# Rearranging the operands of a fused attention, MoE and soft-MoE kernel for 38 prefetch slots

## The chip, the cores and the metric

One core of a Trainium2 chip runs the whole program. The metric is the device time of one execution in microseconds. Its engines are TensorE (PE; its weight loads stand apart as PEld), VectorE (DVE), ScalarE (ACT), GpSimd (POOL) and SyncE (SP), which here issues every transfer. Sixteen DMA engines move the data.

## The reference

Attention over queries pooled in pairs, a two-layer network with ELU on its result, and a soft mixture of eight experts on that (shapes: 4 batches, 8 heads, 1152 positions of 64; 512 model columns; w_in 512 x 2048; phi 512 x 32; w1 8 x 512 x 1024; w2 8 x 1024 x 512):

```python
q_pool = q.reshape(B, H, S // 2, 2, D).mean(axis=3)
attn = softmax(q_pool @ k.T / sqrt(D)) @ v          # to x: 2304 tokens x 512
h = x @ w_in
x = where(h > 0, h, exp(minimum(h, 0)) - 1) @ w_out
logits = x @ phi                                    # 2304 x 32
d = softmax(logits, axis=0)
slot_input = (d.T @ x).reshape(8, 4, 512)           # 4 slots for each expert
for e in range(8):
    slot_out[e] = maximum(slot_input[e] @ w1[e], 0) @ w2[e]
out = softmax(logits, axis=1) @ slot_out.reshape(32, 512)
```

## The kernel before

The kernel does not issue its work directly. Every step is given to a planner (`Plan.add`) with a due time, the engines that may do it, an estimated duration and the buffers it reads and writes. `Plan.run` then deals all steps out: at each turn it takes, of the steps that could start earliest on an engine, the one with the lowest rank (due time plus an offset from `PRI` for its class). What comes out is one fixed program order for each engine; on the chip every engine follows its order and waits on semaphores. A step's class name is phase, buffer name and engine: `1AtaPE` are the token transposes of the last batch (L1038), `1BlgPE` the logits of the last batch (L909).

The work has three phases. *Attention* (phase 0) runs over 16 pairs of heads, until about 427 us. *The two-layer network* (phase 1) consists of 32 products n, each a weight group w with a batch b: n = 0 to 23 run over groups 0 to 7 with batches 0, 1, 2 each, n = 24 to 31 over groups w = 8 to 15 (the same weights again) with batch 3. A product has two halves: `h_mm` (L851, w_in, four blocks of 12 matmuls on psA), then ELU on ACT and DVE, then `o_mm` (L890, w_out, eight groups of 6 matmuls, whose sums DVE adds to X at L901). All groups of a product sum on psC; of the last product (n = 31) four of the eight sum on psA. Each operand is split into a high and a low part. The w_in parts of even w lie in wi, of odd w in wj; the w_out parts of even w in wo, of odd w in wp. H and L are rings of five buffers for the parts of ELU's result; xh and xl the parts of X.

After batch 3 come its logits (L909), column maximum and exponentials, token transposes (L1038, copied into XN tiles by ACT and DVE), the product with the tokens (L1042), and the slot inputs (L1322). `combine` makes, batch by batch, the row softmax (DN), its split C3 (L1084 to L1086) and 20 transposes into C3T (L1105).

*The experts* (phase 2): the weights are 64 blocks of 512 KB, called units: 32 of w1 (rows of 4 KB), then w2, whole for the first experts (rows of 2 KB) and by column halves for the last `NLAST` = 2 (rows of 1 KB; first all of column half m = 0, then m = 1). `load_e` issues a unit on SP (L1215). `stage1` multiplies four w1 units at a time (L1230), `stage2` the w2 units (L1266). `finish(m)` makes column half m of the output: L1279, then nine pairs of token tiles (L1297), scaled into OSB by DVE (L1304) or ACT (L1302), and output transfers (L515) of six tiles each.

The on-chip memory is cut by hand: memr, memf, memv stay, and memy and memz are given up at a swap and taken again as memyq and memzq, once all their earlier users are done. A *slot* is a place of 512 KB for a unit; `spare` declares slots in space that has become free, each with a due time. The first units take the slots in the order of due times; later units (reloads) take them again in turn. Before, there are 29 slots: 4 in memyq, 4 in RAW, 2 each in X0, X1, and X2 (X2 once only), 4 in WR, and 11 in memzq. memy holds x parts of batch 0 alone in phase 1 and is swapped at product 22; memz holds wo, wj, wp, the low part of wi and the parts of batches 1 and 3, and is swapped behind the last L890.

Of the kernel before, what the change touches and what calls it, by code (L numbers as in the profile page):

```python
# [50 lines left out]
class Plan:  # L51
# [66 lines left out]
    def run(self):  # L118
# [54 lines left out]
        for _ in range(n):  # L173
# [41 lines left out]
            if e == "SP":  # L215
                bus = max(st + d + 1.6, bus) + ops[i][7] / 260e3
                end[i] = bus + 0.6
# [34 lines left out]
PRI = {'1AtaPE': -5.3608, '1LTDVE': -0.4594, '1RTDVE': -7.6429, '2SO*': -0.4526, '1MSACT': -0.9307, '1DN*': 8.8491, '2DNACT': 0.2194, '1wph*': -4.7823, '2BePE': -2.9011, '2erSP': -2.9653, '1EmACT': 4.7478, '1wih*': -3.2155, '1SIDVE': -16.5066, '2yqSP': 2.4557, '1Llg*': -8.1331, '2GPool': 3.2101, '2GDVE': -7.1, '2CDVE': 4.4865, '1PH*': 6.0485, '1xn*': -2.6051, '2SELDVE': 3.5395, '2MDVE': -0.6846, '1xl*': 0.61, '1scroSP': 1.1261, '1DRDVE': -0.4279, '2SOP*': -4.7028, '1xnDVE': 0.4531, '2SIZDVE': 6.7579, '1PHDVE': -0.095, '1Lm*': 5.0157, '2zqSP': -4.2858, '2BsitPE': -5.2295, '1BlgPE': 2.9402, '1X*': -1.2546, '2BsoPE': -9.6495, '1BtaPE': 4.0529, '1MSDVE': -5.9118, '2SODVE': 2.4582, '1wil*': -1.2109, '2AePE': -1.6771, '2SIZPool': -1.8218, '2CPE': 0.3788, 'PMXDVE': 5.8326, '0zSP': 5.8562, '0phiSP': 2.4789, '0UA*': -0.3377, 'PnmACT': 7.2492, '0ONERPool': 2.0662, '0qhACT': 0.8522, '0TMPDVE': -0.5015, 'PKRSP': 2.8555, '0QRSP': 2.4444, 'PMZDVE': 0.1661, '0khACT': 3.538, '0RAWACT': -0.5107, '0ACC*': 1.3624, 'PNQDVE': -2.7745, '0SMSP': 1.1984, '0rscrSP': -1.2373, '0scriSP': -4.5893, '0RBSP': 3.284, 'PqhACT': -3.9283, '0NQ*': 0.8442, '0qlDVE': -4.8402, '0KRSP': -0.8079, '0EAACT': 1.6723, 'PkhACT': 4.0482, '0nmACT': 1.1685, '1AhPE': -5.4283, '1wjh*': -0.2497, '1xh*': -9.449, '1woh*': -13.1407, '1wjl*': 1.9459, '1Hlg*': 1.9084, '1Hm*': -1.551, '1XN*': 1.3572, '1scriSP': -0.3405, '1SI*': 5.0824, '1AoPE': -3.7062, '1LT*': -1.0977}  # L252
# [17 lines left out]
OGRP = 6  # L270
# [12 lines left out]
NLAST = 2  # L283
# [3 lines left out]
def attention_moe_softmoe(  # L287
# [65 lines left out]

    def bank(tok):
        return psB[plan.phys[("B",) + tok]]
# [5 lines left out]
    SIZE = {"r": 15232 - 2 * KD * NQ, "f": 24456, "v": ND, "y": KD * NQ * 2, "z": 7 * ND + 2 * KD * NQ}  # L361
# [30 lines left out]
    Hr = [v3(x, 2) for x in carve("r", "H#", 5, NQ)]  # L392
    Lr = [v3(x, 2) for x in carve("r", "L#", 5, NQ)]
# [32 lines left out]
    BW = {("i", 0, x): carve("vz"[x == "l"], "wi" + x, 1, ND, late=True)[0] for x in "hl"}  # L426
    BW.update({("o", 0, x): carve("z", "wo" + x, 1, ND, late=True)[0] for x in "hl"})
# [10 lines left out]
    C3 = carve("r", "C3", 1, len(NT5) * 3 * NS)[0]  # L438
    XN = [v3(x, 2) for x in carve("r", "XN", 1, 2 * DM)]
# [416 lines left out]
    def elu(n, f, t):  # L856
        A, uk, ek, hk, lk = (("A", "h", n, f), ("E", "m", n, f), ("U", "m", n, f), ("H", "m", n, f), ("L", "m", n, f))

        def ph():
# [7 lines left out]
        add(t + 2, ("ACT", "DVE"), (act(NQ), dve2(NQ)), lambda e: copy_(got(Hr, hk), got(Ef, uk))(e), r=[uk], w=[hk])  # L867
        add(t + 2.6, ("DVE", "Pool"), (dve(NQ), pool(NQ)),
            lambda e: sub_(got(Lr, lk), got(Ef, uk), r32(got(Hr, hk)))(e), r=[uk, hk], w=[lk] + ([("elu", f)] if n == NSLOT - 1 else []))

    def o_mm(n, c, t, t0):
# [46 lines left out]
    def logits_split(b, t0):  # L918
        A = ("A", "lg", b)
        for c in range(KD):  # L920
# [4 lines left out]
            def mm(c=c, hk=hk, lk=lk):  # L925
                for x in (got(Hr, hk), got(Lr, lk)):
                    for t in range(2):
                        nc.tensor.matmul(got(psA, A)[: 2 * NS, t, :NH], lhsT=PH[:, c], rhs=x[:, t],
                                         start=(c == 0 and x is got(Hr, hk)), stop=(c == KD - 1 and x is got(Lr, lk)))

            add(t0 + c, ("ACT", "DVE"), (act(NQ), dve2(NQ)), lambda e, src=src, hk=hk: copy_(got(Hr, hk), src)(e), r=xr, w=[hk])
            add(t0 + c + 0.7, ("DVE", "Pool"), (dve(NQ), pool(NQ)),
                lambda e, src=src, hk=hk, lk=lk: sub_(got(Lr, lk), src, r32(got(Hr, hk)))(e), r=xr + [hk], w=[lk])
# [52 lines left out]
    def tok_all(b, t, dt):  # L986
# [38 lines left out]
        add(tq + 1.3, ("ACT", "DVE"), (0.26, 0.24), lambda e: copy_(dn(), pb()[:, :, NS:])(e), r=[tb], w=DK)  # L1025
# [134 lines left out]
    SIZ = over("f", "SIZ", 1, KD * NE * MQ, "LT")[0]  # L1160
    HS = over("f", "HS", 2, HF, "LT", 0, KD * NE * MQ)
    G = over("f", "G", 1, NE * 8 * MQ, "E#")[0]
    SOP = over("f", "SOP", 2, HM, "E#", 0, NE * 8 * MQ)
    SEL = over("f", "SEL", 1, 3 * NS, "E#", 0, NE * 8 * MQ + 2 * HM)[0]
    SO3 = over("r", "SO3", 2, HM, "H#", 0, 4 * ND)
    OSB = v3(over("f", "OSB", 1, NT * HM, "X", 2)[0], NT)
# [5 lines left out]
    def spare(kind, lo, avail, count=1, one=False):  # L1172
        for i in range(count):
            key = (f"er{len(slots_e)}", 0)
            off = lo + i * ND
            plan.region(key, BASE[kind] + off, BASE[kind] + off + ND)
            if one:
                once.add(len(slots_e))
# [11 lines left out]
    spare("z", 0, ts(32.55), 11)  # L1190
# [5 lines left out]
    onek = {f"er{x}" for x in once}  # L1196
# [6 lines left out]
    def load_e(u):  # L1203
# [11 lines left out]
        add(tm + 0.01 * u, "SP", 0.45, lambda: nc.sync.dma_start(v3(t(), a), src), w=[key] + ([("loads", 0)] if u == len(units) - 1 else []), size=524e3)  # L1215
# [4 lines left out]
    def stage1(u, t):  # L1220
# [3 lines left out]
        for i in range(2):  # L1224
# [46 lines left out]
    def finish(m, t):  # L1271
        so, sop = SO3[m], SOP[m]
# [102 lines left out]
```

## Time and profile before

| | us |
|---|---|
| median of 3 runs (lowest, highest) | 997.66 (996.82, 1002.28) |
| the profiled execution | 997.68 |
| its span, first to last instruction | 995.6 |
| PE busy in it | 958.6 |
| DVE busy | 760.4 |
| ACT busy | 496.9 |
| POOL busy | 396.3 |
| read from memory, written | 100.27 MB, 13.18 MB |

Shares of busy time are averages over stages with different limits, so the tail is read by stage. Rows of the timeline give a start, a duration (from the first to the last of a merged run of equal instructions), engine, line, what is written and read, the shape, the count, and in brackets the idle time before it and what ended that. Ends of pipelined matmuls are modelled, so starts are the firmer numbers. Rows of busy time by stage give the stretch, its length, the busy time and instruction count of PE, PEld, DVE, ACT and POOL in it, the clock granted to TensorE (as a share), the mean busy share of the DMA engines, and the GB/s that they moved. Rows of the chain and of the waits say so where they stand.

### The profile page before, as it was taken

What the parts mean: (1) busy time and instruction counts of PE and PEld (TensorE: products, weight loads), DVE (VectorE), ACT (ScalarE), POOL (GpSimd) and SP (SyncE); (2) the same over time, 40 slices, a digit from 0 to 9 for tenths busy, and PEclk for the clock granted to TensorE, in tenths of its full rate; (3) what the DMA queues carried; (4) which work ended last, traced back from release to release, by engine and by line L of the source; (5) the groups of instructions that cost most, each with busy time, mean ns of one, the idle gap of its engine ahead of it and who ended that gap; (6) DMA issues with size and microseconds to landing.
All of it is one profiled execution on the core that took longest, in us unless ns stands there. A gap on an engine that the chain in (4) does not pass through costs nothing.

```text
span 995.6 us, 20896 instructions
## 1 busy us (share of the span) xinstructions
PE 958.6 (96%) x8474; PEld 783.5 (79%) x8474; DVE 760.4 (76%) x1281; ACT 496.9 (50%) x887; POOL 396.3 (40%) x278
## 2 busy tenths in 40 slices
PE   7999999999999999999999999999999999998965
PEld 5777767766777777766899999999999999996423
DVE  6677798888888787899998989989758887765103
ACT  2555566555666566566664444443434475442102
POOL 2878888798888888897200000000000000000000
PEclk7999999999999999999999999999999999998996
DMA  7133424223334342202362332334330132315797
GB/s 175 45 86 85 106 73 122 72 78 113 85 85 116 85 105 61 88 16 67 105 201 89 104 121 95 107 99 162 139 116 28 43 127 86 123 47 230 288 377 267
DMA packets 101583, 114.86 MB, mean 115 GB/s; under 512 B 43632, under 2 KB 70768, under 8 KB 101488
## 3 DMA queue, kind: packets, MB, share of 16 engines
q1 hardware_dynamic: 101488, 113.55, 37.3%
q8 instruction: 66, 1.08, 0.4%
q14 instruction: 29, 0.24, 0.1%
HBM read 100.27 MB, written 13.18 MB: 114 GB/s over the span
## 4 chain that ended last, share of the span: by engine, by line
PE 85%; DVE 8%; DMA 4%; ACT 1%; SPq 1%; issue 1%; DVEq 0%; ACTq 0%
PE psC L890 20%; PE psA L851 20%; PE psC L690 14%; PE psA L683 10%; PE psS L683 5%; PE psA L614 3%; PE psS L614 3%; DVE memf L623 2%; DMA memf<-in_moe_w_dram 2%; PE psC L714 1%; PE psA L598 1%; PE psA L1230 1%; DMA memzq<-in_moe_w_dram 1%; PE psA L575 1%; DVE memf L557 1%; PE psC L659 1%
## 5 line engine op out<-in xcount | busy, mean ns | idle before, releaser
L704 POOL TENSOR_TENSOR memf<-memf 128x576 f32<-128x576 f32 x241 | 360.1, 1496 | 61.4 <-ACT memf L695 35.2
L890 PE MATMUL psC<-memr,memz 128*128 128x288 f32 x1512 | 224.7, 297 | 1.2 <-DVE memf L901 0.7
L890 PEld LDWEIGHTS psC<-memr,memz 128*128 128x128 f32 x1512 | 208.1, 188 | 4.4 <-ACT memf L509 1.6
L690 PE MATMUL psC<-memf 128*64 128x288 f32 x1152 | 174.2, 419 | 0.0
L695 ACT ACTIVATE memf<-psA 128x576 f32<-128x576 f32 x206 | 132.8, 651 | 63.0 <-PE psA L614 54.8
L623 DVE TENSOR_REDUCE memf<-psA 128x2 f32<-128x384 f32 (+3 forms) x235 | 142.5, 618 | 27.6 <-PE psA L614 14.1
L1335 POOL MEMSET memf<- 128x2048 f32 x1 | 1.8, 1809 | 388.4 <-DVE memr L512 388.4
L901 DVE TENSOR_TENSOR memf<-psC,memf 128x288 f32<-128x288 f32 x220 | 100.3, 463 | 47.6 <-PE psC L890 46.0
L623 DVE TENSOR_REDUCE memf<-psS 128x4 f32<-128x768 f32 (+1 forms) x140 | 103.5, 740 | 38.3 <-PE psS L614 20.5
L690 PEld LDWEIGHTS psC<-memf 128*64 128x64 f32 x1152 | 69.8, 136 | 48.6 <-issue 9.3
L851 PE MATMUL psA<-memz 128*128 128x288 f32 x512 | 93.8, 295 | 0.0
L862 ACT ACTIVATE memf<-psA 128x576 f32<-128x576 f32 x64 | 41.8, 652 | 102.8 <-PE psA L851 102.8
L509 ACT CAST memr<-memf 128x576 fp32r<-128x576 f32 x72 | 48.2, 674 | 74.4 <-PE psC L890 35.9
L851 PEld LDWEIGHTS psA<-memz 128*128 128x128 f32 x512 | 76.6, 188 | 0.0
L683 PE MATMUL psA<-memr 64*128 64x288 f32 x816 | 72.1, 299 | 1.8 <-DVE memf L623 1.8
L695 ACT ACTIVATE memf<-psS 128x576 f32<-128x576 f32 x82 | 53.4, 651 | 40.9 <-PE psS L614 35.4
L512 DVE TENSOR_TENSOR memr<-memf,memr 128x576 fp32r<-128x576 f32 x80 | 62.8, 791 | 6.4 <-ACT memr L509 5.9
L683 PEld LDWEIGHTS psA<-memr 64*128 64x128 f32 x816 | 59.1, 185 | 8.6 <-issue 3.9
L683 PE MATMUL psA<-memy 64*128 64x288 f32 x624 | 61.5, 302 | 0.0
L851 PE MATMUL psA<-memz,memv 128*128 128x288 f32 x256 | 52.0, 296 | 0.0
L683 PEld LDWEIGHTS psA<-memy 64*128 64x128 f32 x624 | 47.7, 188 | 4.1 <-issue 3.5
L509 ACT COPY memf<-psC 128x288 f32<-128x288 f32 (+1 forms) x66 | 26.2, 397 | 49.3 <-PE psC L1266 26.7
(209 smaller groups left out, 1602.5 us busy)
## 6 DMA issues: line engine op xcount, KB each, us to landing
memf<-wscr SPq DMA_DIRECT2D x32, 512.0 KB
memf<-in_moe_w_dram SPq DMA_DIRECT2D x30, 512.0 KB
memzq<-in_moe_w_dram SPq DMA_DIRECT2D x22, 512.0 KB
memz<-in_q_dram SPq DMA_DIRECT2D x32, 288.0 KB
memz<-in_k_dram SPq DMA_DIRECT2D x32, 288.0 KB
memf<-in_v_dram SPq DMA_DIRECT2D x16, 576.0 KB
memf<-in_moe_w_in_dram SPq DMA_DIRECT2D x32, 256.0 KB
wscr<-memf SPq DMA_DIRECT2D x32, 256.0 KB
```

The lines of the kernel that those rows point to most:

```text
L509: return lambda e: nc.scalar.copy(out_, in_) if e == "ACT" else nc.vector.tensor_copy(out_, in_)
L512: return lambda e: ENG[e].tensor_tensor(out_, a, b, ALU.subtract)
L614: nc.tensor.matmul(tile_[:m, j, lo : lo + n * MW], lhsT=qkb["qh", i][js, o : o + m], rhs=qkb["kh", i][js, g * MW : (g + n) * MW], start=Tr ...
L623: add(t, "DVE", dve(2 * n * MW), lambda: nc.vector.reduce_max(MX[i][:m, a, :, g : g + n], v4(got(psS, tok)[:m, :, lo : lo + n * MW], n), a ...
L683: nc.tensor.matmul(sp[:, j, :NH], lhsT=qkb[w, i][js, cs] if w else ONER[js], rhs=qkb[m, i][js, hs], start=(x == 0), stop=(x == 3))
L690: nc.tensor.matmul(psC[h][j * D : (j + 1) * D, :NH], lhsT=VR[i][:, j, c], rhs=e[:, j], start=(c == 0), stop=(c == NC - 1))
L695: add(t + 0.01, "ACT", act(NQ, True), lambda: nc.scalar.activation(got(EAf, E_), got(psS, S_)[:, :, :NH], AF.Exp, scale=1.0 / 16.0), r=[S_ ...
L704: ENG[e].tensor_tensor(ac, a, got(EAf, E_), ALU.add)
L851: nc.tensor.matmul(ph[:, t, :NH], lhsT=a, rhs=x, start=(i == 0), stop=(i == 3 * KD - 1))
L862: add(t, "ACT", act(NQ, True), lambda: nc.scalar.activation(got(Ef, uk), ph(), AF.Relu, scale=-1.0), r=[A], w=[uk])
L890: nc.tensor.matmul(po_(), lhsT=a, rhs=x, start=(i == 0), stop=(i == 3 * GF - 1))
L901: add(t0 + 0.8, "DVE", dve(NH), lambda: nc.vector.tensor_tensor(d, po_(), d, ALU.add), r=[ck], w=XK)
```

## The change

- The memory is cut anew. memy grows to 14 slots and holds, in phase 1, the parts of batches 0, 1 and 3 and wi's low part, wo and wj; memz shrinks and holds wp and the rings H and L. memyq is swapped with a due time behind the last w_in product (`YSW` = 31.2) and gives 14 slots, memzq 7. One more slot lies beside G in the E buffers, two (once only) in X3: 38 in all.
- DN of batches 0 to 2 moves into LT, C3T's space is shared with the last batch's XN tiles, HS and SOP move.
- The output gets a buffer for each column half (OS0 over X2 and X3, OS1 in memzq) and other transfer sizes: up to tiles 2, 6, 12, 18 for m = 0, and 6, 12, 16, 18 for m = 1.
- `NLAST` = 4: four experts by column halves, 16 half units instead of 8.
- `PRI` puts the last batch's logits ahead of its token transposes. In the planner, loads of phase 2 count 0.67 of their size instead of 0.75, and steps on SP without bytes no longer take up the bus.

```diff
-PRI = {'1AtaPE': -5.3608, ... '1BlgPE': 2.9402, ...
+PRI = {'1AtaPE': 4.0, ... '1BlgPE': -4.0, ...
-OGRP = 6
+OGRP = [[2, 6, 12, 18], [6, 12, 16, 18]]
-NLAST = 2
+NLAST = 4
+YSW = 31.2
...
-    SIZE = {"r": 15232 - 2 * KD * NQ, "f": 24456, "v": ND, "y": KD * NQ * 2, "z": 7 * ND + 2 * KD * NQ}
+    SIZE = {"r": 15232 - 2 * KD * NQ - 10 * NQ, "f": 24456, "v": ND, "y": KD * NQ * 4 + 5 * ND, "z": 2 * ND + 10 * NQ}
...
-    Hr = [v3(x, 2) for x in carve("r", "H#", 5, NQ)]
-    Lr = [v3(x, 2) for x in carve("r", "L#", 5, NQ)]
+    zo = 2 * ND
+    Hr = carve("z", "H#", 5, NQ, off=zo, late=True)
+    Lr = carve("z", "L#", 5, NQ, off=zo + 5 * NQ, late=True)
...
-    BW = {("i", 0, x): carve("vz"[x == "l"], "wi" + x, 1, ND, late=True)[0] for x in "hl"}
-    BW.update({("o", 0, x): carve("z", "wo" + x, 1, ND, late=True)[0] for x in "hl"})
...
-    BW.update({("i", 1, x): carve("z", "wj" + x, 1, ND, late=True)[0] for x in "hl"})
+    BW = {("i", 0, x): carve("vy"[x == "l"], "wi" + x, 1, ND, late=True)[0] for x in "hl"}
+    BW.update({("o", 0, x): carve("y", "wo" + x, 1, ND, late=True)[0] for x in "hl"})
+    BW.update({("i", 1, x): carve("y", "wj" + x, 1, ND, late=True)[0] for x in "hl"})
     BW.update({("o", 1, x): carve("z", "wp" + x, 1, ND, late=True)[0] for x in "hl"})
-    XH[1], XL[1] = (carve("z", f"x{x}1", 1, KD * NQ, late=True)[0] for x in "hl")
+    XH[1], XL[1] = (carve("y", f"x{x}1", 1, KD * NQ, late=True)[0] for x in "hl")
...
-        kind, off = ("v", 0) if i == 0 else ("r", plan.base[("H#", 0)][0] - BASE["r"] + (i - 1) * 2 * DM)
+        kind, off = ("v", 0) if i == 0 else ("r", plan.base[("C3T", 0)][0] - BASE["r"] + (i - 1) * 2 * DM)
...
-    OSB = v3(over("f", "OSB", 1, NT * HM, "X", 2)[0], NT)
+    OS0 = v3(over("f", "OS0", 1, NT * HM, "X", 2)[0], NT)
+    plan.region(("OS1", 0), BASE["z"] + oz, BASE["z"] + oz + NT * HM)
...
-    swap("y", y_es, "yq", ts(22.2))
-    spare("y", 0, ts(22.3), 4)
+    swap("y", y_es, "yq", ts(YSW))
+    spare("y", 0, ts(YSW + 0.05), 14)
...
     swap("z", z_es, "zq", ts(32.5))
-    spare("z", 0, ts(32.55), 11)
+    spare("z", 0, ts(32.55), 7)
+    spare("f", pos("E#") + NE * 8 * MQ, ts(32.5), r=[("elu", 0), ("elu", 1)])
+    spare("f", pos("X", 3), tm2 + 9, 2, True)
```

## Rows read from the trace of the kernel before

**Rows 1.** The page: DMA share (tenths) and GB/s of 40 slices.
```profile
DMA  7133424223334342202362332334330132315797
GB/s 175 45 86 85 106 73 122 72 78 113 85 85 116 85 105 61 88 16 67 105 201 89 104 121 95 107 99 162 139 116 28 43 127 86 123 47 230 288 377 267
```

**Rows 2.** Busy time by stage, columns as told under the table above.
```profile
440.00:480.00 40.00, 37.85 (x352) 28.38 (x349) 37.35 (x36) 26.25 (x46) 31.46 (x19) 1.00 0.12 41
...
920.21:925.83 5.62, 4.91 (x36) 2.41 (x38) 2.11 (x8) 1.59 (x7) 0.00 (x0) 0.90 0.14 56
...
938.00:978.00 40.00, 29.73 (x286) 13.53 (x287) 3.25 (x21) 3.45 (x11) 0.00 (x0) 0.89 1.01 358
978.00:995.60 17.60, 7.88 (x51) 5.41 (x49) 7.64 (x13) 6.13 (x15) 0.00 (x0) 0.69 0.79 268
```

**Rows 3.** The chain that ended last, from 923 on: start us, us, what.
```profile
936.16 10.76 DMA memf<-in_moe_w_dram
...
964.08 9.55 DMA memf<-in_moe_w_dram
```

**Rows 4.** Timeline of SP from 735 on.
```profile
905.21 7.39 SPq L1215 DMA_DIRECT2D memzq<-in_moe_w_dram  x11
925.83 1.75 SPq L1215 DMA_DIRECT2D memyq<-in_moe_w_dram  x4
...
979.24 10.42 SPq L515 DMA_DIRECT2D out_dram<-memf  x6
```

**Rows 5.** Busy time by stage again, for its last columns, DMA share and GB/s.
```profile
915.21:920.21 5.00, 4.49 (x11) 2.10 (x11) 1.16 (x5) 2.56 (x12) 0.00 (x0) 0.50 1.03 414
...
980.00:985.00 5.00, 3.53 (x25) 2.60 (x21) 3.55 (x7) 2.44 (x7) 0.00 (x0) 1.00 0.94 315
...
990.00:994.40 4.40, 0.00 (x0) 0.00 (x0) 0.00 (x0) 0.00 (x0) 0.00 (x0) 0.50 0.96 329
```

**Rows 6.** Timeline of PE from 955 on: expert products and what they waited for.
```profile
963.45 1.06 PE L1266 MATMUL psC<-memzq,memf 128*32 128x256 f32 x12 [0.73 <-DMA memzq<-in_moe_w_dram]
...
966.17 1.06 PE L1266 MATMUL psC<-memzq,memf 128*32 128x256 f32 x12 [0.74 <-DMA memzq<-in_moe_w_dram]
967.68 0.64 PE L1266 MATMUL psC<-memyq,memf 128*32 128x256 f32 x8 [0.45 <-DMA memyq<-in_moe_w_dram]
...
973.67 1.08 PE L1266 MATMUL psC<-memf 128*32 128x256 f32 x8 [0.71 <-DMA memf<-in_moe_w_dram]
```

**Rows 7.** Timeline of PE from 885 on: the last products of the network.
```profile
889.26 1.76 PE L851 MATMUL psA<-memz 128*128 128x288 f32 x12
890.86 1.75 PE L890 MATMUL psC<-memr,memz 128*128 128x288 f32 x12
...
896.08 0.97 PE L890 MATMUL psA<-memr,memz 128*128 128x288 f32 x6
...
898.55 1.06 PE L890 MATMUL psC<-memr,memz 128*128 128x288 f32 x6 [0.70 <-DVE memf L901]
899.45 0.97 PE L890 MATMUL psA<-memr,memz 128*128 128x288 f32 x6
```

**Rows 8.** Timeline from 905 to 947: tokens, slots and C3 on PE and DVE.
```profile
905.01 1.03 PE L1038 MATMUL psA<-ident,memf 128*64 128x128 f32 x8
...
920.36 1.29 PE L1105 MATMUL psB<-ident,memr 128*96 128x128 f32 x4
...
923.89 1.92 PE L1230 MATMUL psA<-memyq,memf 128*32 128x512 f32 x16
...
942.10 0.32 DVE L1084 CAST memr<-memf 128x160 fp32r<-128x160 f32 x1 [1.71 <-PE psB L1105]
...
945.07 1.36 PE L1105 MATMUL psB<-ident,memr 128*96 128x128 f32 x4
```

**Rows 9.** Waits of SP (us in all, times, longest); a DVE row.
```profile
SPq L515 <- DVE memf L1304: 15.7, 6, 8.2
...
985.68 1.29 DVE L1304 TENSOR_TENSOR memf<-psA,memf 128x512 f32<-128x512 f32 x2 [0.18 <-DMA out_dram<-memf]
```

More of the change, by code (lines that the diff above doesn't have):

```diff
@@ L214, in run @@
                 port = st + d
-            if e == "SP":
+            if e == "SP" and ops[i][7]:
                 bus = max(st + d + 1.6, bus) + ops[i][7] / 260e3
@@ L925, in mm @@
             def mm(c=c, hk=hk, lk=lk):
[L926 removed]
+                for k, x in enumerate((hl(Hr, hk), hl(Lr, lk))):
                     for t in range(2):
                         nc.tensor.matmul(got(psA, A)[: 2 * NS, t, :NH], lhsT=PH[:, c], rhs=x[:, t],
[L929 to L931 removed]
+                                         start=(c == 0 and k == 0), stop=(c == KD - 1 and k == 1))
+            add(t0 + c, ("ACT", "DVE"), (act(NQ), dve2(NQ)), lambda e, src=src, hk=hk: copy_(hl(Hr, hk), src)(e), r=xr, w=[hk])
             add(t0 + c + 0.7, ("DVE", "Pool"), (dve(NQ), pool(NQ)),
[L933 removed]
+                lambda e, src=src, hk=hk, lk=lk: sub_(hl(Lr, lk), src, r32(hl(Hr, hk)))(e), r=xr + [hk], w=[lk])
             add(t0 + c + 1.5, "PE", pe(4 * NH), mm, r=[hk, lk, ("PH", 0)], w=[A])
@@ L1024, in tok_all @@
         add(tq + 1.2, "DVE", 0.5, d_split, r=[tb], w=[("DR", 0)])
-        add(tq + 1.3, ("ACT", "DVE"), (0.26, 0.24), lambda e: copy_(dn(), pb()[:, :, NS:])(e), r=[tb], w=DK)
+        add(tq + 1.3, ("ACT", "DVE"), (0.26, 0.24), lambda e: copy_(dn(), pb()[:, :, NS:])(e), r=[tb], w=DK + ([("LT", 0, 0, h) for h in range(2)] if b < B - 1 else []))
         for i, (o, n) in enumerate(nt):
@@ L1158, in over, with hs, osb @@
         return carve(kind, name, n, size, off=pos(old, oi, kind) + skip)
-    SIZ = over("f", "SIZ", 1, KD * NE * MQ, "LT")[0]
-    HS = over("f", "HS", 2, HF, "LT", 0, KD * NE * MQ)
-    G = over("f", "G", 1, NE * 8 * MQ, "E#")[0]
-    SOP = over("f", "SOP", 2, HM, "E#", 0, NE * 8 * MQ)
-    SEL = over("f", "SEL", 1, 3 * NS, "E#", 0, NE * 8 * MQ + 2 * HM)[0]
-    SO3 = over("r", "SO3", 2, HM, "H#", 0, 4 * ND)
-    OSB = v3(over("f", "OSB", 1, NT * HM, "X", 2)[0], NT)
+    SIZ = over("f", "SIZ", 1, KD * NE * MQ, "LT", 0, LD)[0]
+    HS1 = carve("f", "HS", 1, HF, off=pos("LT") + LD + KD * NE * MQ, first=1)[0]
+    plan.region(("HS", 0), BASE["z"] + 7 * ND, BASE["z"] + 7 * ND + HF)
+    def hs(i):
+        return HS1 if i else MEM["z"][:, 7 * ND : 7 * ND + HF]
+    G = over("f", "G", 1, NE * 8 * MQ, "E#")[0]
+    SEL = over("f", "SEL", 1, 3 * NS, "E#", 0, NE * 8 * MQ + ND)[0]
+    for i in range(2):
+        plan.region(("SOP", i), BASE["z"] + 7 * ND + i * HM, BASE["z"] + 7 * ND + (i + 1) * HM)
+    SO3 = over("r", "SO3", 2, HM, "XN")
+    OS0 = v3(over("f", "OS0", 1, NT * HM, "X", 2)[0], NT)
+    oz = 0
+    plan.region(("OS1", 0), BASE["z"] + oz, BASE["z"] + oz + NT * HM)
+    def osb(m):
+        return v3(MEM["z"][:, oz : oz + NT * HM], NT) if m else OS0
     SIZv = SIZ.rearrange("p (c e m) -> p c e m", c=KD, m=MQ)
@@ L1170, in attention_moe_softmoe, with spare @@
     slots_e, once = [], set()
-    def spare(kind, lo, avail, count=1, one=False):
+    behind = {}
+    def spare(kind, lo, avail, count=1, one=False, r=()):
         for i in range(count):
@@ L1195, in attention_moe_softmoe @@
     units += [(3, e, m, k) for m in range(2) for e in range(NE - NLAST, NE) for k in range(2)]
-    onek = {f"er{x}" for x in once}
+    onek = once
     slot_of, prev, ring = list(range(NSL)), {}, [u for u in range(NSL) if slots_e[u][0][0] not in onek]
@@ L1271, in finish, with sop @@
     def finish(m, t):
-        so, sop = SO3[m], SOP[m]
+        so = SO3[m]
+        def sop():
+            return MEM["z"][:, 7 * ND + m * HM : 7 * ND + (m + 1) * HM]
         tk = ("B", "so", m)
@@ L1276, in ps @@
             return got(psB, tk)[: 3 * NS, :HM]
-        add(t, ("ACT", "DVE"), (act(HM, True), dve(HM)), lambda e: copy_(sop, psC[m][:, :HM])(e), r=[("C", m)], w=[("SOP", m)])
-        add(t + 0.4, "PE", 0.45, lambda: nc.tensor.matmul(ps(), lhsT=SEL, rhs=sop, start=True, stop=True), r=[("SOP", m), ("SEL", 0)], w=[tk])
+        add(t, ("ACT", "DVE"), (act(HM, True), dve(HM)), lambda e: copy_(sop(), psC[m][:, :HM])(e), r=[("C", m)], w=[("SOP", m)])
+        add(t + 0.4, "PE", 0.45, lambda: nc.tensor.matmul(ps(), lhsT=SEL, rhs=sop(), start=True, stop=True), r=[("SOP", m), ("SEL", 0)], w=[tk])
         add(t + 0.9, ("ACT", "DVE"), (act(HM, True), dve(HM)), lambda e: copy_(so[: 3 * NS], ps())(e), r=[tk], w=[("SO3", m)])
```

44 lines of the change are left out of this document (24 added, 20 removed).

## The prediction

> **What bounds the kernel now.** I read the slices of the page first. TensorE is busy in nine tenths of nearly every slice until the last few, and the DMA engines are filled only in the last four or five [rows 1]. The busy time by stage says the same with sharper edges: in 440 to 480 us TensorE lacks 2.15 us, and between 938 and 978 the DMA engines are full (share 1.01) while TensorE has 10 us to spare [rows 2]. So the kernel has two parts: some 900 us bound by TensorE, which this change hardly edits, and a tail bound by the 64 expert blocks of 512 KB. The chain of waits confirms it: from 936 on it consists of landings of expert blocks [rows 3].
>
> The queue of SyncE shows the tail as a transfer schedule [rows 4]. 29 blocks are prefetched; the last eleven go out at 905.21, when the w_out buffers come free. The other 35 reload slots and go out from 925.83, when the first expert product has released four slots. Between the eleven and the 35 the DMA engines run dry (share 0.14 from 920.2 to 925.8 [rows 2]). The six output transfers start at 979.24.
>
> **Prices.** A block of w1 (rows of 4 KB) at 414 GB/s takes 524,288 B / 414 = 1.27 us [rows 5]. Whole blocks of w2 (rows of 2 KB) reach TensorE in pairs, 966.17 - 963.45 = 2.72 us apart, so 1.36 each; half blocks (rows of 1 KB) come four in 973.67 - 967.68 = 5.99 us, so 1.50 each [rows 6]. First test on the kernel before: from 925.83 to 973.67 blocks 29 to 60 arrive: 3 of w1, 24 whole, 5 halves = 3.8 + 32.6 + 7.5 = 43.9 us of 47.8. The missing 3.9 us are what a stream costs from its first issue until it flows. The last three halves bring block 63 to 973.67 + 4.5 = 978.2. From there to the end of the span are 17.4 us.
>
> By the Trainium skill (DMA: Bandwidth & Descriptors, Specifications) transfers run at line rate from 512 B on, so that rows of 1 KB would cost nothing. Rows 5 and 6 disagree: 1.27, 1.36 and 1.50 us for the same bytes. By the page the sixteen halves of the new kernel would take 16 x 1.36, 2.2 us less than I count.
>
> **The change, part by part.** *38 slots.* Only 26 blocks reload instead of 35. Sorted by due time, RAW, X0, X1, WR take blocks 0 to 11, memyq 12 to 25, E# 26, memzq 27 to 33, X3 34 and 35, X2 36 and 37. The four memyq blocks that were loaded at leisure long before are now loaded late with ten others; what counts is when memy comes free. Memy now holds wo as well, the w_out buffer of even weight groups, and the last but one product (n = 30, w = 14) is even. After the last product with w_in (the L851 group at 889.26) sixteen groups of six L890 matmuls follow [rows 7]: twelve on psC and four on psA. Only the last product (n = 31) uses psA, four times, and psC four times; so eight psC groups, the whole of product 30, run behind the last w_in product. They rank ahead of product 31, so I take the first eight psC groups: the row at 890.86 holds the first two, and the one at 898.55, which waited for DVE, is the eighth (five groups of six and one of product 31 lie between). The next group starts at 899.45. Memy is then free at 899.5 rather than at 891.0, and at 905.0 at worst, if one group of product 30 is left to the end.
>
> *The stream from 899.5.* In queue order: 14 blocks for memyq, E#, seven for memzq, two for X3, then 26 reloads. 20 of these are w1, 4 + 10 whole, 16 halves: 3.9 + 20 x 1.27 + 14 x 1.36 + 16 x 1.50 = 3.9 + 25.4 + 19.0 + 24.0 = 72.3 us, provided that nothing in it waits. Memzq's slots are free at 905 and X3 after its transposes at about 915, both long before their turn (the memyq blocks alone take until 921). The reloads need the first L1230 products. The prefetch runs dry at 899.5 + 3.9 + 25.4 + 5.4 = 934.2; a reload must be issued 3.9 us earlier, at 930.3; before, the first issue came 1.94 us behind the first L1230 (923.89 [rows 8]). So L1230 may start as late as 928.4 without cost. Block 63 is then there at 899.5 + 72.3 = 971.8, 6.4 us earlier than now.
>
> *Four experts by halves.* Eight more blocks at 1.50 instead of 1.36: 1.1 us, contained in the sum. In exchange the first half of the output is finished early: its last block is eight halves (12 us) ahead of the last load instead of four (6 us).
>
> *Output.* The first output transfer waited 8.2 us for DVE L1304, the scaling of its blocks, not for the loads [rows 9]; and the second half's scaling waited for output transfers to leave the one OSB buffer (the DVE row at 985.68 [rows 9]). With OS0 and OS1 apart, and 12 us of lead against the 7 us that the first six blocks took behind the last block of their half (973.67 - 1.50 = 972.2, to 979.24), the first half's transfers stand in the queue behind the last load, and data flow on without a gap. The bytes are the same, 4.72 MB, and took from 980.0 to 994.4 (14.4 us at 315 to 329 GB/s [rows 5]); 1.2 us follow. So the end is 971.8 + 14.4 + 1.2 = 987.4 against 995.6. The second half's first chunk must be ready within half of the 14.4 us; before, with the conflicts, it took 985.6 - 978.2 = 7.4, so at worst 1 us of gap.
>
> *Logits ahead of token transposes.* The 20 transposes (8 take about 1.0 us: L1038 at 905.01 [rows 8], so 2.5 in all) leave the way of the logits, and their copies on ACT and DVE move into it: a gain between 0 and 2.5 us for the first L1230, or a loss of as much if DVE is late for the column maximum. On the path it counts nothing: there are 4.5 us of cover (928.4 - 923.9) in the stream.
>
> *Combine.* C3T now lies under the last batch's XN tiles, so all 20 L1105 transposes and their DVE splits stand behind the last token product (which ends when L1105 begins at 920.36 [rows 8]), where before some were done earlier. They end by about 950 at the pace of rows 8 (one batch from 942.10 to 946.4), and the first use is the first half's output at about 960. Cover: the loads. On the first L1230 they could cost up to the whole four batches, below.
>
> *At nothing:* H, L, wp in memz, wi's low half, wo, wj, x1 in memy: the same number of buffers and the same copies; DN in LT, HS, SOP and SEL elsewhere; the scheduler's rate for phase 2 (0.67) changes the order only. The order of the first 900 us may be dealt anew: at most the 2.15 us that TensorE lacks around 460 are to be won [rows 2], with DVE at 37.35 of 40 about as much to be lost.
>
> **The sum.** Span 987.4, and 997.68 - 995.6 = 2.1 around it: 989.5 us, 8.2 under the profiled execution, which equals the median of the runs (997.66).
>
> **Rivals.** (1) Memy free at the last w_in product, as the change is described: issue at 891.2, block 63 at 963.5 if L1230 starts by 920.1; it will start between 921.5 and 923.9, so 1.4 to 3.8 us late: 982.6 to 985.0. Against it: the L890 order of rows 7. (2) Memy free only with the last group of all, or the whole prefetch behind it: stream from 905.2, 5.7 us later: 995.2, no measurable change. For it: product 30 and 31 are mixed there; against it: rank. (3) Outputs held until the last load has landed, or the second half late: 0.9 to 1.5 us more, 990.4 to 991. (4) Slower: the program order on TensorE puts the four combine batches ahead of the first L1230. At 4.6 us each from 920.5 the first L1230 would stand at about 940, 11.6 us beyond 928.4: 1001. It decides from 928.4 on, and the kernel is slower than before once L1230 starts beyond 936.6. For it: all 20 transposes now become ready there; against it: before, seven stood between 920.36 (four of them [rows 8]) and 923.89 and L1230 went ahead of the other seven. (5) The first 900 us dealt anew: plus or minus 2 us, or in a bad case 4.
>
> **Chances.** Forecast 60% (989.5, own range 987 to 992); rival 1 10%, rival 2 11%, rival 3 10%, rival 4 4%, rival 5 beyond 2 us 5%. A measurement of this kernel tells about 0.5%, 5 us, from no change: 992.7 and 1002.6 are the bounds. Faster 0.81 (forecast, rivals 1 and 3, parts of 5), same 0.16 (rival 2, parts of 4 and 5), slower 0.03. The range from 984.5 to 995.5 leaves out most of rival 1 and the cases above.
>
> **What would show it.** In the queue of SyncE: 14 memyq issues from about 899.5 (rival 1: 891; rival 2: 905), 26 reloads instead of 35, no dry stretch in the DMA share from 901 to the end. TensorE's waits for blocks end with halves 1.50 apart, the last at about 972. Output transfers of the first half issued before that, the second half from about 978. L1230 between 921.5 and 924, without effect on the end. Wrong is the sum if DMA idles anywhere after 901, or if the stage before 899 is itself shifted by more than 2 us.

## The result, and the profile after

The changed kernel took 989.78 us (median of 5; 988.25 to 991.08) against 998.56 us for the kernel before on the same chip: ratio 0.9903, 95% interval 0.988 to 0.9926. A second measurement on another chip gave 990.3 against 999.78, ratio 0.9912 (0.9897 to 0.9928). The forecast was 989.5. The profiled execution of the changed kernel is the fastest of the five: 988.25 us, with a span of 986.4.

The queue of SyncE in the changed kernel answers [rows 4]. Columns: start, duration from the first to the last issue of a merged run, engine, line, transfer, count. L1237 issues expert blocks (it was L1215), L1337 the outputs (L515).

```profile
894.03 2.47 SPq L1237 DMA_DIRECT2D memf<-in_moe_w_dram  x2
900.92 12.35 SPq L1237 DMA_DIRECT2D memyq<-in_moe_w_dram  x14
914.26 7.99 SPq L1237 DMA_DIRECT2D memzq<-in_moe_w_dram  x7
923.22 19.12 SPq L1237 DMA_DIRECT2D memf<-in_moe_w_dram  x14
942.43 22.82 SPq L1237 DMA_DIRECT2D memyq<-in_moe_w_dram  x14
966.84 4.22 SPq L1337 DMA_DIRECT2D out_dram<-memf  x4
977.05 4.25 SPq L1337 DMA_DIRECT2D out_dram<-memzq  x4
```

The fourteen memyq blocks start at 900.92, not with the last w_in product at 891.6. The timeline of PE shows why (L856 is w_in, L895 w_out; the bracket is the idle time before, and what ended it):

```profile
891.63 1.76 PE L856 MATMUL psA<-memy 128*128 128x288 f32 x12
893.24 5.18 PE L895 MATMUL psC<-memz,memy 128*128 128x288 f32 x36
898.26 0.95 PE L895 MATMUL psA<-memz 128*128 128x288 f32 x6
899.05 1.84 PE L895 MATMUL psC<-memz,memy 128*128 128x288 f32 x12
...
906.38 4.09 PE L914 MATMUL psB<-memf,phi_sb 128*64 128x288 f32 x16
...
924.83 7.13 PE L1252 MATMUL psA<-memf 128*32 128x512 f32 x48
...
971.00 0.64 PE L1288 MATMUL psC<-memyq,memf 128*32 128x256 f32 x8 [0.82 <-DMA memyq<-in_moe_w_dram]
972.44 0.64 PE L1288 MATMUL psC<-memyq,memf 128*32 128x256 f32 x8 [0.80 <-DMA memyq<-in_moe_w_dram]
```

Behind the last L856 group stand eight w_out groups that read memy (36 + 12 matmuls, product 30); they end at about 900.9. The list of SyncE's waits names them too (us in all, times, longest):

```profile
SPq L1237 <- PE psC L895: 4.3, 1, 4.3
```

The first expert product begins at 924.83, and the last block reaches TensorE at 972.44.

Busy time by stage (stretch, its length, busy time and count of PE, PEld, DVE, ACT, POOL, the clock granted to TensorE, DMA share, GB/s) answers [rows 2, 5]:

```profile
905.00:924.00 19.00, 15.74 (x76) 9.85 (x75) 9.41 (x28) 6.96 (x23) 0.00 (x0) 0.85 1.02 407
924.00:938.00 14.00, 13.76 (x110) 3.71 (x114) 0.00 (x0) 1.86 (x5) 0.00 (x0) 0.84 1.04 391
938.00:972.00 34.00, 28.85 (x345) 15.69 (x337) 7.69 (x31) 8.47 (x29) 0.00 (x0) 1.00 1.08 359
...
975.00:980.00 5.00, 3.73 (x18) 3.22 (x18) 3.37 (x6) 3.24 (x8) 0.00 (x0) 0.62 0.69 236
```

The DMA engines are full from 905 to 972. The dry stretch of the kernel before (share 0.14 [rows 2]) is gone. The rate falls with the rows: 407 GB/s for rows of 4 KB, 359 for a stretch that is mostly rows of 1 KB. Behind the loads a new gap opens: from 975 to 980 the share is 0.69, between the first half's output transfers and those of the second half, which are issued only at 977.05.

### The profile page after: what moved, and what is told of

Its sections match the earlier page's. It is cut to its first block, busy times and chain, and to the rows that moved or that the text cites. A ratio compares the mean times of both kernels' runs of the same rounds, so it can differ in the third digit from the quotient of the medians.

```text
span 986.4 us, 20905 instructions
## 1 busy us (share of the span) xinstructions
PE 952.2 (97%) x8474; PEld 781.8 (79%) x8474; DVE 762.0 (77%) x1275; ACT 499.1 (51%) x894; POOL 397.1 (40%) x278
## 3 DMA queue, kind: packets, MB, share of 16 engines
q8 instruction: 66, 1.08, 0.5%
## 4 chain that ended last, share of the span: by engine, by line
PE 85%; DVE 9%; DMA 2%; ACT 1%; issue 1%; SPq 0%; ACTq 0%; DVEq 0%
PE psC L895 20%; PE psA L856 20%; PE psC L695 13%; PE psA L688 10%; PE psS L688 4%; DVE memf L628 3%; PE psS L619 3%; PE psA L619 3%; DMA memyq<-in_moe_w_dram 2%; PE psA L1252 2%; PE psC L719 1%; PE psA L603 1%; DVE memy L517 1%; PE psA L580 1%; PE psC L1288 1%
## 5 line engine op out<-in xcount | busy, mean ns | idle before, releaser
L856 PE MATMUL psA<-memy 128*128 128x288 f32 x768 | 140.3, 294 | 0.0
L895 PE MATMUL psC<-memz,memy 128*128 128x288 f32 x768 | 115.3, 296 | 0.9 <-ACT memf L514 0.9
L856 PEld LDWEIGHTS psA<-memy 128*128 128x128 f32 x768 | 114.9, 188 | 0.0
L895 PE MATMUL psC<-memz 128*128 128x288 f32 x744 | 111.4, 296 | 0.0
L895 PEld LDWEIGHTS psC<-memz,memy 128*128 128x128 f32 x768 | 106.0, 188 | 3.5 <-ACT memf L514 2.1
L695 PEld LDWEIGHTS psC<-memf 128*64 128x64 f32 x1152 | 69.8, 136 | 48.6 <-issue 9.3
L895 PEld LDWEIGHTS psC<-memz 128*128 128x128 f32 x744 | 102.7, 188 | 0.7 <-DVE memf L906 0.2
L514 ACT CAST memz<-memf 128x576 fp32r<-128x576 f32 (+1 forms) x77 | 54.3, 713 | 79.3 <-PE psC L895 39.5
L856 PE MATMUL psA<-memy,memv 128*128 128x288 f32 x384 | 77.8, 296 | 0.0
L517 DVE TENSOR_TENSOR memz<-memf,memz 128x576 fp32r<-128x576 f32 (+1 forms) x84 | 68.4, 819 | 9.3 <-ACT memz L514 9.0
L856 PEld LDWEIGHTS psA<-memy,memv 128*128 128x128 f32 x384 | 61.2, 188 | 0.6 <-issue 0.6
```

Of the source, the lines that this page charges most:

```text
L514: return lambda e: nc.scalar.copy(out_, in_) if e == "ACT" else nc.vector.tensor_copy(out_, in_)
L517: return lambda e: ENG[e].tensor_tensor(out_, a, b, ALU.subtract)
L695: nc.tensor.matmul(psC[h][j * D : (j + 1) * D, :NH], lhsT=VR[i][:, j, c], rhs=e[:, j], start=(c == 0), stop=(c == NC - 1))
L856: nc.tensor.matmul(ph[:, t, :NH], lhsT=a, rhs=x, start=(i == 0), stop=(i == 3 * KD - 1))
L895: nc.tensor.matmul(po_(), lhsT=a, rhs=x, start=(i == 0), stop=(i == 3 * GF - 1))
```

## The experiments

Twelve runs in three groups of four; each group shares a chip and its runs of the kernel before (1000.36, 999.78 and 999.93 us). Only the second group holds a run of the changed kernel itself; elsewhere the ratios are what compares. Executions of these kernels differ by up to 3.0 us already at the first w_in product (460.74 in the changed kernel, 463.70 with wo in memz and the old ranks), although the order of TensorE's work up to there is the same, so beside the times the table has two numbers of the profiled execution that are free of that: when the first reload is issued, counted from the first memyq issue, and how long the span lasts from that issue. (The profiled execution is the fastest one for the changed kernel and for wo in memz, first run, 988.25 and 984.97 us, and the slowest one for the second run of wo in memz and for wo in memz with the old ranks, 990.66 and 991.28.)

| kernel | median us | ratio to before (95%) | memyq issue | first reload after | to the end |
|---|---|---|---|---|---|
| changed kernel | 989.78 | 0.9903 (0.988, 0.9926) | 900.92 | 27.6 | 85.5 |
| the same again | 990.3 | 0.9912 (0.9897, 0.9928) | 902.85 | 26.0 | 86.0 |
| 36 slots | 991.31 | 0.9916 (0.9903, 0.9929) | 903.62 | 27.9 | 85.7 |
| old ranks | 991.01 | 0.9911 (0.9897, 0.9924) | 903.68 | 26.7 | 85.8 |
| one output buffer | 990.68 | 0.9909 (0.9894, 0.9923) | 903.70 | 27.6 | 85.2 |
| two experts by halves | 992.42 | 0.9932 (0.992, 0.9944) | 902.91 | 26.0 | 87.7 |
| both of these | 992.27 | 0.9924 (0.9909, 0.9939) | 902.69 | 27.9 | 87.3 |
| batch 1's split held | 991.35 | 0.9914 (0.99, 0.9927) | 903.17 | 27.3 | 86.3 |
| wo in memz | 986.03 | 0.9869 (0.9849, 0.9888) | 894.43 | 32.9 | 88.7 |
| the same again | 986.74 | 0.9867 (0.9846, 0.9887) | 896.74 | 35.2 | 92.1 |
| wo in memz, old ranks | 987.99 | 0.9887 (0.9868, 0.9907) | 897.23 | 35.9 | 92.3 |
| wo in memz, split held | 988.04 | 0.9884 (0.9869, 0.9899) | 895.01 | 34.1 | 91.0 |
| before, 27 slots | 1002.6 | 1.0025 (1.0013, 1.0038) | | | |

**What frees memy.**

```diff
-    BW.update({("o", 0, x): carve("y", "wo" + x, 1, ND, late=True)[0] for x in "hl"})
+    BW.update({("o", 0, x): carve("z", "wo" + x, 1, ND, late=True)[0] for x in "hl"})
...
-    spare("y", 0, ts(YSW + 0.05), 14)
+    spare("y", 0, ts(YSW + 0.05), 12)
...
-    spare("z", 0, ts(32.55), 7)
+    spare("z", 0, ts(32.55), 9)
```

> The changed kernel with one buffer pair moved: the w_out parts of even weight groups (wo) lie in memz instead of memy, so that memy gives 12 slots and memz 9; the 38 slots, the order of work on PE, ACT and DVE up to the tail stay. Theory A (what frees memy is the last product that reads wo, product 30, and the end is set by the stream of blocks that starts there): the memyq issues move from 900.92 us to just behind the last L856 group, about 893.3; the stream flows until the prefetch is used up, then runs dry until the first expert product releases slots (928.49 in the changed kernel, 4 us or so after it would be wanted), so of the 7.6 us about 3 are won: about 987 us where the changed kernel has 990. Theory B (the issue waits for something else, such as the rank of the loads or the last group of all): issues still at about 900.9, no difference (within 0.5 us).

> The kernel with wo in memz once more, as the base for the run with the old ranks beside it and to see whether its gain over the changed kernel holds on another chip. Both theories: ratio to the kernel before 0.987 (0.985 to 0.989), where the changed kernel had 0.990 and 0.991.

Measured: 986.03 and 986.74 us. The product that reads memy last is now the last w_in product (it starts at 891.64 and takes 1.8 us), and the issues follow it by 1.0 us, behind one block for memf that stands ahead of them in SyncE's queue and went out at 894.05 (timeline of SyncE, first run of this kernel):

```profile
894.43 9.94 SPq L1237 DMA_DIRECT2D memyq<-in_moe_w_dram  x12
```

That is 6.5 us earlier than in the changed kernel. The end gains less, 3.4 to 4.5 us by the ratios (0.9903 and 0.9912 against 0.9869 and 0.9867), because the prefetch now runs out before the first expert product releases slots. In the stretch around the first reload the engines are not quite full any more in the first run, and they run dry in the second, where the first expert product began later (rows of the one, then of the other):

```profile
925.00:930.00 5.00, 5.00 (x36) 1.24 (x32) 0.00 (x0) 0.00 (x0) 0.00 (x0) 0.65 0.96 335
```

```profile
930.00:935.00 5.00, 5.00 (x44) 1.28 (x40) 0.00 (x0) 0.00 (x0) 0.00 (x0) 0.89 0.48 164
```

Theory A holds: product 30 held memy, and it is the moment of release that sets the end, until the first expert product takes over. This kernel beats the changed kernel as well as the one before. Its interval clears that of the changed kernel measured again (0.9897 to 0.9928) and just overlaps that of its first measurement.

**How much a slot is worth.** Two slots fewer, in the changed kernel and in the kernel before:

```diff
-    spare("z", 0, ts(32.55), 7)
+    spare("z", 0, ts(32.55), 5)
```

```diff
-    spare("z", 0, ts(32.55), 11)
+    spare("z", 0, ts(32.55), 9)
```

> The changed kernel with 5 instead of 7 slots in memzq, so 36 slots in all and 28 reloads instead of 26. Theory A (prediction: what counts is a stream without a dry stretch from the moment when memy is free; a slot counts only if the prefetch would end before the first expert product releases slots; there were 4.5 us of cover in the sum, two blocks take 2.5): no difference, within 0.7 us, and the DMA engines dry for at most 1 us ahead of the first reload. Theory B (each slot saves one load time behind the products): 2 x 1.3 = 2.6 us slower.

> The kernel before with 9 instead of 11 slots in memzq, so 27 slots in all. Theory A (prediction: there the DMA engines run dry between the prefetch and the first reload, so that every missing slot puts one more load behind the first expert product): 2 blocks by 1.3 us, 2.5 to 2.7 us slower than the kernel before, while the same edit on the changed kernel cost at most 1 us. Theory B (the tail of the kernel before starts with the prefetch, not with the first product): no difference, within 0.7 us.

Measured: in the changed kernel 991.31 beside 990.3, intervals overlapping, and 85.7 us from the memyq issue to the end where the unedited kernel has 85.5 and 86.0. In the kernel before 2.7 us more (1002.6 against 999.93; by the interval 1.3 to 3.8), about two blocks at 1.3 us. In the profiles the last block reaches TensorE 56.0 us behind the first reload with 27 slots and 53.7 with 29, so 2.3 us of it are a longer stream of reloads. The stage rows say why. With 36 slots the engines stay almost full around the first reload at 931.5; in the kernel before with 27 they stand still for most of ten microseconds (rows of the one, then of the other):

```profile
930.00:935.00 5.00, 5.00 (x48) 1.40 (x44) 0.00 (x0) 0.00 (x0) 0.00 (x0) 0.91 0.95 352
```

```profile
920.00:925.00 5.00, 4.37 (x19) 2.68 (x21) 2.23 (x8) 1.69 (x7) 0.00 (x0) 0.50 0.00 1
925.00:930.00 5.00, 5.00 (x32) 1.15 (x28) 0.00 (x0) 0.00 (x0) 0.00 (x0) 0.62 0.15 30
```

So a slot is worth a load time where the stream runs dry behind the prefetch, and next to nothing where it does not. The 36 and the 38 slots are both enough.

**Logits ahead of token transposes.** The two ranks put back, in the changed kernel and in the one with wo in memz:

```diff
-PRI = {'1AtaPE': 4.0, ... '1BlgPE': -4.0, ...
+PRI = {'1AtaPE': -5.3608, ... '1BlgPE': 2.9402, ...
```

> The changed kernel with the old ranks of the last batch: token transposes ahead of logits. Theory A (prediction: the first expert product has some 4 us of cover in the stream of blocks, so the rank counts nothing on the path): the first w1 product starts up to 2.5 us later, block 63 and the end stay, within 0.5 us. Theory B (logits first is what lets the reloads start in time): DMA runs dry ahead of the first reload and the end is 2 us later or more.

> The kernel with wo in memz (12 and 9 slots), and with the old ranks, token transposes ahead of logits. There memy is free 6.5 us earlier and the prefetch is used up just about when the first reload is issued (927.3 us). Theory A (logits first shortens the way to the first expert product, and now nothing covers it): first product and first reload 1 to 2.5 us later, the end 1 to 2 us later than with logits first. Theory B (logits first does not make the first expert product earlier; in the changed kernel it began 18.4 us behind the last w_out group with it and 17.8 without): no difference, or up to 0.6 us faster.

Measured: 991.01, 85.8 us from issue to end: no difference, theory A of the first. The first expert product itself begins 17.8 us behind the last w_out group with the old ranks (926.81 - 909.05) and 18.45 us with the new (924.83 - 906.38), but these two executions do not compare: over this way the granted clock was 0.90 in the one and 0.82 in the other. In the second measurement of the changed kernel, where it was 0.91, the way took 16.9 us (925.24 - 908.32). At about equal clock, then, logits first gains some 0.8 us of the 2.5 that were possible. The timeline of the changed kernel shows where more of it goes: the last four transposes are late, and the last two token products wait for their copies.

```profile
916.69 1.79 PE L1047 MATMUL psC<-memr 128*64 128x512 f32 x4
918.33 0.60 PE L1043 MATMUL psA<-ident,memf 128*128 128x128 f32 x4
...
919.58 0.69 DVE L1053 TENSOR_TENSOR memr<-psA,memr 128x512 fp32r<-128x512 f32 x1 [2.56 <-ACT memr L514]
...
919.60 0.45 PE L1047 MATMUL psC<-memr 128*64 128x512 f32 x1 [0.68 <-ACT memr L514]
...
920.32 0.44 PE L1047 MATMUL psC<-memr 128*64 128x512 f32 x1 [0.28 <-DVE memr L1053]
```

With wo in memz, where nothing covers the first expert product, the old ranks cost 1.25 us by the medians (987.99 against 986.74) but the intervals overlap widely: this stays open.

**Four experts by halves, and two output buffers.**

```diff
-NLAST = 4
+NLAST = 2
```

```diff
-        return v3(MEM["z"][:, oz : oz + NT * HM], NT) if m else OS0
+        return OS0
```

> The changed kernel with two experts by column halves (NLAST 2) instead of four: eight blocks of w2 come whole (1.36 us each) instead of as sixteen... eight halves (1.50 us each). Theory A (prediction: the halves cost 1.1 us of loading and buy the first output half a lead of 12 us instead of 6): block 63 lands 1.1 us earlier, but the first half's scaling is late, so the output transfers start behind a gap of 1 to 2 us: within 1 us of the changed kernel, either side. Theory B (the lead is worth nothing): 1.1 us faster.

> The changed kernel with both column halves of the output scaled into one buffer (OS0), as the kernel before had it; OS1 stays unused. Theory A (prediction: buffers apart keep the second half's scaling from waiting for the first half's transfers): the second half's output transfers are issued 1.5 to 2.5 us later and the end with them. Theory B (the first half's transfers leave early enough with 12 us of lead): no difference, within 0.5 us.

> The changed kernel with two experts by halves and with one output buffer, the two edits of which the first cost 2.1 us and the second nothing. Theory A (a buffer of its own for the second half only matters where the first half is late; with 12 us of lead it is not): here the first output transfer is issued at about 974, so the second half's scaling waits for transfers that are still under way, and this kernel is 1 to 2.5 us slower than the one with two experts by halves alone (992.42 us), about 994. Theory B (the buffers never mattered): as that one, within 0.5 us.

Measured: two experts by halves instead of four cost 2.1 us (992.42 against 990.3). The intervals of the two ratios touch (from 0.992 on the one side, up to 0.9928 on the other), but from the memyq issue to the end both kernels with two take 87.3 and 87.7 us where the six with four and wo in memy take 85.2 to 86.3. One output buffer costs nothing, alone (990.68 against 990.3) or with two experts by halves (992.27 against 992.42). The first is more than either theory had; the mechanism is that of theory A. With two experts by halves the loads thin out from about 971 on, but the products with block 63 start only at 974.11, without a wait for it: they stand in TensorE's order behind the first half's output products. In the changed kernel measured beside it, whose memyq issue lies within 0.1 us, they start at 974.27, so the shorter loading gains nothing there. And the first output is issued only at 974.22, where that one had it at 968.65. Queue and stages of the kernel with two experts by halves:

```profile
974.22 4.28 SPq L1337 DMA_DIRECT2D out_dram<-memf  x4
...
965.00:970.00 5.00, 3.15 (x29) 0.72 (x26) 0.00 (x0) 0.37 (x1) 0.00 (x0) 0.63 1.09 348
970.00:975.00 5.00, 5.00 (x36) 2.27 (x37) 1.92 (x4) 1.40 (x4) 0.00 (x0) 0.69 0.28 89
975.00:980.00 5.00, 3.47 (x21) 2.44 (x20) 3.67 (x7) 2.77 (x8) 0.00 (x0) 0.99 0.95 325
```

Between loads and outputs the DMA engines are at 0.28. In the changed kernel (first measurement) that stretch is full, with the end of the loads and then the first half's outputs:

```profile
970.00:975.00 5.00, 2.13 (x22) 0.56 (x18) 0.32 (x1) 0.74 (x2) 0.00 (x0) 1.00 1.09 382
```

So the lead is what pays. It doesn't close every gap: the changed kernel has its own from 975 to 980 (share 0.69, above), which is smaller. The output's transfer sizes, changed along with it, were not varied. The conflict over one buffer does occur (with both edits one scaling waits for a transfer), but it is half a microsecond behind transfers that keep the engines at 0.98 to 0.99, so it costs nothing. Theory A fell in both runs that gave the second buffer a price. Timeline of DVE and stage row of the kernel with both edits:

```profile
982.21 1.29 DVE L1330 TENSOR_TENSOR memf<-psB,memf 128x512 f32<-128x512 f32 x2 [0.49 <-DMA out_dram<-memf]
...
980.00:985.00 5.00, 2.27 (x11) 1.98 (x9) 2.95 (x5) 1.82 (x5) 0.00 (x0) 0.50 0.99 338
```

**Why the network stage runs late.** The products of the changed kernel begin 2.1 to 2.5 us later than before in the two profiled executions. That is partly luck: the execution of the kernel before ran longer at the lower clock near the start (granted 0.65 from 20 to 30 us, against 0.80) and was 1.2 us behind at 34 us (the same eight matmuls at 34.51 and 33.35), so counted from there the network starts 3.4 us later (2.9 against the kernel before with 27 slots). The shift arises between 230 and 365 us, in the attention, where the split of batch 1's x (ACT L514, DVE L517 into memy) now stands; before, its space was shared with memz and it came after memz's swap.

```diff
-        add(t, ("ACT", "DVE"), (act(NQ), dve2(NQ)), lambda e: copy_(part(0), src)(e), r=S_, w=[xk("h", b, c)])
+        add(t, ("ACT", "DVE"), (act(NQ), dve2(NQ)), lambda e: copy_(part(0), src)(e), r=S_ + ([("z", 0)] if b == 1 else []), w=[xk("h", b, c)])
```

> The changed kernel with one added dependence: the high parts of batch 1's x wait for the swap of memz, as they did before the change through the space that they shared. Theory A (the network of the changed kernel runs 2.4 us late because this split, 576 columns by ACT and DVE each, was pulled into the attention stage, where DVE is nearly full): the network's products come 2.4 to 3.5 us earlier than in the changed kernel, the memyq issues at about 898.5, the tail is unchanged behind them, total about 2.4 us less (987.4). Theory B (the shift is only how the two executions differed): issues within 0.7 us of 900.92 and the same time.

> The changed kernel with both edits: wo in memz (12 and 9 slots) and batch 1's split behind the swap of memz. Theory A of both: the two gains add, 2.4 + 3 us, about 984.5 us. If the split's shift is hidden (the stream waits for the first expert product and not for memory), the gains still add, since that product moves with the network. Rival: one gain alone, 987.

Measured: 991.35, no gain; with wo in memz 988.04, no gain either (986.03 without it). The origin is right: from 230 to 300 us, in the kernel before, the changed one, and the one with the split held, in this order, DVE has 57.4, 62.3 and 57.5 us of work and TensorE 69.8, 67.4 and 69.7:

```profile
230.00:300.00 70.00, 69.81 (x741) 49.83 (x739) 57.36 (x91) 42.31 (x74) 60.33 (x42) 1.00 0.34 85
```

```profile
230.00:300.00 70.00, 67.39 (x706) 47.36 (x704) 62.34 (x90) 40.87 (x72) 60.16 (x41) 1.00 0.35 93
```

```profile
230.00:300.00 70.00, 69.68 (x740) 49.63 (x737) 57.48 (x90) 42.04 (x74) 60.30 (x41) 1.00 0.34 85
```

But the work does not vanish when it is held: TensorE then loses 1.3 us against the other two between 300 and 365 (63.38 against 64.66 of 65), and between 440 and 520 another 1.0 to 1.5 us (75.30 busy against 76.29 in the changed kernel and 76.78 before). Its last w_in group starts 1.36 us behind the changed kernel's, of which 1.06 us were there from 31 us on, so 0.3 us later where 2.4 earlier was expected. The other profiles say the same. The first w_in group starts between 460.74 and 463.70 in the ten executions with this split in the attention, at 460.00 and 459.43 in the two with it held, at 458.50 and 458.06 in the kernel before with 29 and with 27 slots. From there to the last w_in group it takes 430.7 to 430.9 us in the first ten and in the last two, and 433.0 and 432.8 with the split held. So holding it gives the attention some of its time back, and the network, whose order is dealt anew, loses 2.1 us. My expectation that the shift could be undone this way fell.

## Point by point

- **Release of memy at 899.5, behind product 30**: right in kind, 900.92 in the profile. Of the 1.4 us too late, 2.4 come from the shifted network, and 1.0 is regained because [rows 7] had a stall behind DVE that this execution lacks (the run measured again has it, and issues at 902.85). Rival 1 (free at the last w_in product) needs wo elsewhere; with wo in memz it happens, and gave 986.0 and 986.7 where the rival had 982.6 to 985.0. The issue came at 894.43 instead of 891.2, and the first product at 923.65 in one execution, within the rival's range, and at 928.86 in the other.
- **Stream of 72.3 us**: 900.92 to 972.44 is 71.5. The sum had one block too many in it, 1.27 us: 15 blocks instead of 14 went out ahead of the memyq blocks, the last two from 894.03 on. The others took 0.5 us longer than counted. The steps of 1.27, 1.36 and 1.50 us hold; the last two halves reach TensorE 1.44 us apart (972.44 - 971.00). The Trainium skill's rule that transfers run at line rate from 512 B on (DMA: Bandwidth & Descriptors, Specifications) does not agree with this trace either: 407 GB/s for rows of 4 KB against 348 for rows of 1 KB alone (965 to 970 with two experts by halves). The measurement decides.
- **Cover of 4.5 us for the first expert product**: enough, but smaller than thought. The first reload came 3.66 us behind the first product (924.83 to 928.49) where the sum took 1.94 from the kernel before; there this stretch had the full clock (granted 1.00), here half of it (0.50). First reloads between 26.0 and 27.9 us behind the memyq issue give the same end (85.2 to 86.3 us), with 36 slots too.
- **Output, 15.6 us from block 63 to the end**: measured 14.0 (986.4 - 972.44). The size was off by 1.6 us, and the mechanism was not the one forecast. All 4.72 MB were to flow behind the last load without a gap. Instead the first half's outputs, issued from 966.84 on, were nearly through at 976, and then the DMA engines waited (0.69 from 975 to 980, so some 1.6 us idle) for the second half's first transfer at 977.05, 4.6 us behind block 63. From there to the end it took 9.4 us, in both measurements. What ends the kernel is thus the second half's way from block 63 through its scaling and its own transfers. By the prediction's own sign ("Wrong is the sum if DMA idles anywhere after 901") this step failed, and the early start of the first half more than made up for it. The reason given was half right too: the lead of 12 us is worth the 2.1 us that two experts by halves lose; OS0 and OS1 apart, which the sum named beside it, are worth nothing.
- **Four experts by halves, +1.1 us**: contained in the stream. In the changed kernel the halves are a net gain.
- **Logits first, 0**: right on the path; of the 0 to 2.5 us of gain for the first product some 0.8 are there at equal clock.
- **Combine at cover, no harm**: three L1110 transposes stand ahead of the first L1252 product, from 923.44 on, and the others lie between 940 and 958. It was read from the trace and not tried alone. Rival 4 did not come about.
- **"At nothing" for x1 in memy**: the step that was mis-sized. The network came 2.4 us later than in the profile of before, 3.4 without that execution's slow start, beyond the 2 us that the prediction named as its second sign of a wrong sum. Release (+1.4), stream (-0.8) and output (-1.6) add to -1.0, so the span came out at 986.4 instead of 987.4. Both signs showed and the number still held, because errors on both sides cancelled: that is luck.

## What to carry to other kernels

Where a stream of loads sets the end, its first issue counts: look which reader gives its space back last, and move that one operand. A prefetch slot has a price only where the stream runs dry behind it; look for the dry stretch before adding slots. Cutting the last loads so that outputs can start before loading ends paid more than the slower rows cost.

## What the runs showed of the hardware

**Output rows of one size left at two rates.** Rows of 1 KB are read at 348 GB/s and the second half's outputs, also rows of 1 KB, are written at 338 (rows above). The first half's outputs of the changed kernel flow faster. In its second measurement block 63 reaches TensorE at 974.27, so behind that no load is under way, and yet:

```profile
975.00:976.00 1.00, 0.60 (x2) 0.24 (x2) 0.00 (x0) 0.35 (x1) 0.00 (x0) 1.00 1.09 386
976.00:977.00 1.00, 0.09 (x2) 0.01 (x1) 0.42 (x1) 0.37 (x1) 0.00 (x0) 0.83 1.08 384
```

So the 382 GB/s of the row of 970 to 975 above need no mix of reads and writes: the outputs alone reach as much. With wo in memz the same half's outputs, issued when the loads were nearly through, move at 326 to 355 in each microsecond from 967 to 973. What makes the difference was not tried.

**TensorE's clock makes the first expert product vary.** With wo in memz the same four token matmuls, in the same program order, began 9.5 us behind the start of the logits in one execution, and took 1.08 us (916.79 on); in the other they began 10.3 us behind and took 1.91 us (919.95 on). The rows of 910 to 925 of the first and then of the second execution show the clock beside it:

```profile
910.00:915.00 5.00, 3.83 (x30) 2.62 (x29) 2.10 (x6) 3.07 (x7) 0.00 (x0) 1.00 1.02 406
915.00:920.00 5.00, 3.86 (x18) 1.92 (x17) 3.45 (x11) 3.34 (x13) 0.00 (x0) 1.00 1.03 410
920.00:925.00 5.00, 3.81 (x20) 2.00 (x23) 2.13 (x8) 1.19 (x7) 0.00 (x0) 0.66 1.03 397
```

```profile
910.00:915.00 5.00, 4.70 (x24) 2.65 (x22) 1.38 (x5) 1.17 (x3) 0.00 (x0) 1.00 1.03 409
915.00:920.00 5.00, 4.13 (x23) 2.37 (x24) 3.78 (x11) 2.89 (x8) 0.00 (x0) 0.75 1.03 411
920.00:925.00 5.00, 4.08 (x11) 1.85 (x9) 1.27 (x5) 2.83 (x12) 0.00 (x0) 0.50 1.02 402
```

In the first the clock stays at 2.4 GHz (share 1.00) until 920, in the second it is at 1.2 GHz (0.50) from 920 to 925 and for part of the stretch before. In the two stretches from 910 to 920 TensorE was busy for 3.83 and 3.86 us of 5 in the first and for 4.70 and 4.13 in the second, which is 2.3 us further back in its program. The first expert product began 16.4 us behind the last w_out group in the one (923.65 - 907.29) and 19.25 us in the other (928.86 - 909.61), and this kernel's executions spread from 985.0 to 990.7 us. In all ten profiles with logits first, whose order on TensorE is the same here, this way goes with the mean clock granted over it: 16.4 us at 0.94, 16.9 at 0.90 and 0.91, 18.25 to 18.5 at 0.82 and 0.83, 19.2 at 0.70 and 0.71. In the changed kernel the stream covers such a difference. What makes the clock fall at different moments was not tried.
